# Weight conversion in lagged stages, a later P2, and two sums moved to VectorE, in a fused attention and FFN kernel

## The chip, the cores and the metric

The kernel runs on one core of one Trainium2 chip. The metric is the time of one execution on the device in microseconds (us), the median of several runs. The core has five engines that matter here: TensorE (PE, with its weight loads as PEld), VectorE (DVE), ScalarE (ACT), GpSimd (POOL) and SyncE (SP), which here only issues DMAs.

## The reference

Attention with normalised queries and keys, and then a feed-forward layer with squared ReLU:

```
q_n, k_n = rmsnorm(q) * g_q, rmsnorm(k) * g_k         # (8, 12, 448, 64) f32
attn = softmax(q_n @ k_n.T / sqrt(64))
x = (attn @ v) laid out as (8 * 448, 768)
h = maximum(x @ w_in, 0.0)                            # w_in (768, 2048)
out = (h * h) @ w_out                                 # w_out (2048, 768)
```

w_in and w_out arrive as float64; q, k, v and the output are float32.

## The kernel before

The work is cut into four units of two batches. The order of all instructions is written out by hand (`tc.manual_schedule`), and each engine executes its own in that order; the waits between engines come from the tiles that they share. A unit has 48 steps. A step belongs to one pair of heads i (12 pairs in a unit, 4 steps n = 0 to 3 in a pair) and issues the scores and exponentials of pair i (`weigh`, lines 205 and 207) and the products with the values of pair i - 1 (`attend`, line 260, with the row sums on line 267 or 271 and their reciprocal `rden` on line 282). Around these stand `normalize` for pair i + 2 (lines 156 to 166: the mean squares `ms` on DVE, the power `rr` and the product `qn` on POOL), `turn` for pair i + 1 (transposes on line 185, then `qT` on DVE at n = 0 and `kT` on ACT at n = 2) and `finish` for pair i - 2 (`xT` on line 292). Where batch 1 of a unit reaches its last three pairs, `finish` also makes the forms T1 to T4 of x (`make_x_forms`, line 317).

In unit 0 attention runs alone and the weights are converted beside it: 64 pieces of 384 KB, four to every three steps. `convert(n)` does three things: `join_words(n - 1)` (three DVE operations, lines 558 to 566), `load_weights(n + 4)` (one DMA into `words`, seven buffers) and `split_words(n)` (three ACT operations, lines 541 to 548, and a clamp on POOL, line 542). Whenever the fourth piece of a tile of weights is joined, `make_weight_forms` issues four chained sums on POOL (line 583) and one DMA on SP that writes the tile with its sums to DRAM (`in_forms`, `out_forms`, line 584). Pieces come as two tiles of w_in, two of w_out, and so on.

From step 4 of units 1, 2 and 3 on, the FFN of the unit before is spread between the attention steps (`ffn`, paced by `spent`); that of the last unit stands alone at the end. It is a Strassen-Winograd scheme with seven products for each 2 by 2 block. In each of four blocks, two tiles of `first_products` (line 383; seven products of six matmul instructions each) fill `hid`, where `hidden` adds on DVE (402), applies ReLU on ACT (403) and squares on POOL (404); then `second_products` does the rows that both batches share (line 420, 16 matmul instructions), makes four sums of `hid` on POOL (line 438), and runs three row tiles of seven products (line 448). Four PSUM banks, `roles`, take the products: P1, P6 and P7 use role 0, P5 and P3 role 1, P2 role 2, P4 role 3. `turn_roles` gives the next tile the banks of the old roles 2, 3, 1, 0 in this order, so that the next P1 writes the bank that held P2. The other banks are 0 and 1 for scores, 2 for transposes and row sums and 3 for the products with the values; in unit 0 attention has all eight.

At the end of each FFN `store` issues 14 DMAs on SP, ahead of the loads of the next unit.

Of the kernel before, what the change touches and what calls it, by code (L numbers as in the profile page):

```python
# [1 line left out]

# [11 lines left out]
ALU = mybir.AluOpType  # L14
# [59 lines left out]
def program(ctx, tc, q, k, v, g_row, moe_w_in, moe_w_out, out, shift):  # L74
# [35 lines left out]


    pairs = [(b, c) for b in range(B) for c in range(NPAIR)]
    loaded, values, squared, normal, turned = {}, {}, {}, {}, {}
    weights, sums, dens, xts, forms = {}, {}, {}, {}, {}

    def alone(i):

        return pairs[i][0] < 2

    def load_qk(i):  # L120
        b, c = pairs[i]
# [74 lines left out]
    def weigh(i, m):  # L196

        if shift:
            return weigh_shifted(i, m)
        new_weights(i, m)  # L200
        qT, kT = turned[i, 0], turned[i, 1]
        scs = [banks[(2 * (m % 2) if alone(i) else 0) + e][:CP, 0:S] for e in range(2)]
        for e, sc in enumerate(scs):
            r = ds(e * D, D)
            nc.tensor.matmul(sc, lhsT=kT[r, ts(m, CP)], rhs=qT[r, :], start=True, stop=True)  # L205
        for e, sc in enumerate(scs):
            nc.scalar.activation(  # L207
                weights[i, e, m], sc, AF.Exp, scale=normal[i][2][:, 2 * m + e : 2 * m + e + 1]
            )
        add_up(i, m)  # L210
# [35 lines left out]
                add_up(i, n)  # L246

    def values_bank(i):
        return banks[4 + i % 2 if alone(i) else 3][:, 0:S]

    def attend(i, m):

        av = values_bank(i)
        den = banks[6 + i % 2 if alone(i) else 2][:, 0:S]
        for e in range(2):
            nc.tensor.matmul(  # L260
                av[ds(e * D, D), :], lhsT=values[i][:, e, m, :], rhs=weights[i, e, m],
                start=m == 0, stop=m == NJ - 1,
            )
        for e in range(2):
            wT = weights.pop((i, e, m))
            if alone(i):
                nc.tensor.matmul(
                    den[ds(e * D, D), :], lhsT=ones, rhs=wT, start=m == 0, stop=m == NJ - 1
                )
            elif m == 1:  # L270
                nc.tensor.matmul(  # L271
                    den[ds(e * D, D), :], lhsT=ones, rhs=sums.pop((i, e)), start=True, stop=True
                )
        if m == (NJ - 1 if alone(i) else 1):
            rden = att.tile([P, S], F32, name="rden", tag="rden", bufs=1)
            if shift:
                nc.vector.tensor_scalar(
                    out=rden, in0=den, scalar1=1e-9, scalar2=None, op0=ALU.add
                )
                nc.vector.reciprocal(out=rden, in_=rden)  # L280
            else:
                nc.vector.reciprocal(out=rden, in_=den)  # L282
            dens[i] = rden
# [28 lines left out]
    def make_x_forms(u, c):  # L312
        b11, b12, b21, b22 = [xts.pop((2 * u + e, c + NK * a)) for a in range(2) for e in range(2)]
        t1, t2, t4 = new_x(), new_x(), new_x()
        t3 = b12
        for dst, left, right in (t1, b12, b11), (t2, b22, t1), (t3, b22, b12), (t4, t2, b21):
            nc.gpsimd.tensor_tensor(out=dst, in0=left, in1=right, op=ALU.subtract)
        forms[u, c] = {"11": b11, "21": b21, "22": b22, "T1": t1, "T2": t2, "T3": t3, "T4": t4}

    IN = ["11", "12", "S3", "22", "S1", "S2", "S4"]  # L320
# [21 lines left out]
    def turn_roles():  # L342
# [1 line left out]
        roles[:] = w, y, v_, x  # L344


    ORDER = [
        ("P1", 0, True, "11", "11"), ("P5", 1, True, "S1", "T1"), ("P2", 2, True, "12", "21"),
        ("P6", 0, False, "S2", "T2"), ("P4", 3, True, "22", "T4"), ("P3", 1, False, "S4", "22"),
        ("P7", 0, False, "S3", "T3"),  # L350
    ]
    COST_IN, COST_OUT = 12 * NK // 2, 10
    COST = NF // 2 * 7 * COST_IN + NBLK * (NT * 7 + 4) * COST_OUT

# [19 lines left out]
    def first_products(u, p, hid):  # L374

        turn_roles()
        n = u * NF // 2 + p
        w_sb = in_sb.pop(n)
        copies = {}
        for name, role, first, left, right in ORDER:  # L380
            ps = roles[role][:, 0:S]
            for c in range(NK):
                nc.tensor.matmul(  # L383
                    ps, lhsT=w_sb[:, c, IN.index(left), :], rhs=forms[u, c][right],
                    start=first and c == 0, stop=c == NK - 1,
                    skip_group_check=not first,
                )
            if name in ("P1", "P5", "P6", "P4"):
                copies[name] = ffn_p.tile([P, S], F32, name="part", tag="part", bufs=4)
                nc.scalar.copy(copies[name], ps)  # L390
            elif name == "P2":
                hidden(hid[0][:, 0], ps, copies["P1"], ALU.add)
            elif name == "P3":
                hidden(hid[0][:, 1], ps, copies["P6"], ALU.add)
            elif name == "P7":
                hidden(hid[1][:, 0], ps, copies["P4"], ALU.subtract)
                hidden(hid[1][:, 1], ps, copies["P5"], ALU.add)
                load_in(n + 2)
            yield COST_IN

    def hidden(dst, ps, part, op):
# [4 lines left out]
    def second_products(u, blk, hid, accs):  # L406
# [4 lines left out]
        ns = [u * NF // 2 + 2 * blk + t for t in range(2)]  # L411
        w_sb = [out_sb[n] for n in ns]


        turn_roles()
        for half in range(2):
            ps = roles[half][:, 0:HALF]
            for a in range(2):
                for t in range(2):
                    nc.tensor.matmul(  # L420
                        ps, lhsT=flat[a][:, t, ds(FULL, P)], rhs=w_sb[t][:, 2 * a + half, :],
                        start=a == 0 and t == 0, stop=a == 1 and t == 1,
                    )
            add_to(accs[-1][:, ts(half, HALF)], ps, blk == 0)
            yield 2 * COST_OUT

        sums_ = [
            ffn_p.tile([P, 2, FULL], F32, name="sums", tag=f"S{n}", bufs=1) for n in range(3)
        ]
# [1 line left out]
        a11, a12 = [a[:, :, lower] for a in flat]  # L431
        a21, a22 = [a[:, :, upper] for a in flat]
        s3 = a21
        for dst, left, right, op in (
            (s1, a21, a22, ALU.add), (s2, s1, a11, ALU.subtract),
            (s3, a11, a21, ALU.subtract), (s4, a12, s2, ALU.subtract),
        ):
            nc.gpsimd.tensor_tensor(out=dst, in0=left, in1=right, op=op)  # L438
        lefts = {"11": a11, "12": a12, "22": a22, "S1": s1, "S2": s2, "S3": s3, "S4": s4}
        for tt in range(NT):  # L440
            turn_roles()
            upper_acc, lower_acc = accs[2 * tt], accs[2 * tt + 1]
            c11, c12 = [upper_acc[:, ts(h, HALF)] for h in range(2)]
            c21, c22 = [lower_acc[:, ts(h, HALF)] for h in range(2)]
            for name, role, first, left, right in ORDER:
                ps = roles[role][:, 0:HALF]
                for t in range(2):
                    nc.tensor.matmul(  # L448
# [47 lines left out]

    def weight_pieces():

        for blk in range(NBLK):
            for p in range(2 * blk, 2 * blk + 2):  # L500
                for form, (a, b) in enumerate(((0, 0), (1, 0), (0, 1), (1, 1))):
                    yield "in", p, form, moe_w_in[ds(a * HALF, HALF), ts(p + b * NF // 2, P)]
            for t in range(2 * blk, 2 * blk + 2):
                for form in range(4):
                    a, b = divmod(form, 2)
                    yield "out", t, form, moe_w_out[ts(t + a * NF // 2, P), ts(b, HALF)]

    all_pieces = list(weight_pieces())
    words, low_words, targets = {}, {}, {}

    def target(n):
        kind, t, form, rows = all_pieces[n]
# [61 lines left out]
    def make_weight_forms(kind, dst, t):  # L574
        add, sub = ALU.add, ALU.subtract
        if kind == "in":
            a11, a12, a21, a22, s1, s2, s4 = [dst[:, :, n, :] for n in range(7)]
            todo = (s1, a21, a22, add), (s2, s1, a11, sub), (a21, a11, a21, sub), (s4, a12, s2, sub)
        else:
            b11, b12, b21, b22, t1, t2, t3, t4 = [dst[:, n, :] for n in range(8)]  # L580
            todo = (t1, b12, b11, sub), (t2, b22, t1, sub), (t3, b22, b12, sub), (t4, t2, b21, sub)
        for to, left, right, op in todo:
            nc.gpsimd.tensor_tensor(out=to, in0=left, in1=right, op=op)  # L583
        nc.sync.dma_start((in_forms if kind == "in" else out_forms)[t], dst)

    def convert(n):

        join_words(n - 1)
        load_weights(n + 4)
        split_words(n)  # L590

    load_qk(0)
    for n in range(2):
# [12 lines left out]

    last = len(pairs) - 1
    unit_steps = 2 * NPAIR * NJ  # L610

    with tc.manual_schedule(engines=ENGINES):
# [8 lines left out]
        for i, (b, c) in enumerate(pairs):  # L621
            u = b // 2
            for n in range(NJ):
# [6 lines left out]
                    load_qk(i + 3)  # L630
                if step == NJ and u:
                    stream, spent = ffn(u - 1), 0
                    if u == 1:
                        for t in range(2):
                            load_in(t)
                            load_out(t)
                while u and (
                    shift and step == NJ and spent < COST
                    or spent * (unit_steps - NJ) < COST * (step - NJ + 1)
# [15 lines left out]
                if u == 0:  # L655
                    while 3 * piece < 4 * (step + 1):
                        convert(piece)
                        piece += 1
                elif u == 1 and step == 0:
                    convert(piece)  # L660
            if b % 2 and c == NPAIR - 1:
                for _ in stream:
                    pass
# [37 lines left out]
```

## Time and profile before

| what | value |
|---|---|
| median of 3 runs | 1765.96 us (1765.89 to 1767.84) |
| the profiled execution | 1768.41 us |
| its span, first to last instruction | 1766.5 us |
| busy, share of span: PE, POOL, DVE, ACT | 89%, 40%, 42%, 31% |
| mean granted TensorE clock | 0.952 of full |

The trace is of one execution. Busy times of one engine may overlap a little with its idle times, because the ends of matmuls are modelled. A granted clock of 1.00 is 2.4 GHz, and 0.50 is 1.2 GHz.

### The profile page before, as it was taken

How to read it: one execution, taken by the hardware profiler on the slowest of the kernel's cores; microseconds unless marked ns; L12 is line 12 of the kernel's file. 1: busy time of each engine (PE TensorE's matmuls, PEld its weight loads, DVE VectorE, ACT ScalarE, POOL GpSimd, SP SyncE). 2: the span in 40 equal slices, each digit the busy share in tenths (PEclk: the TensorE clock that was granted, in tenths of full speed). 3: DMA queues.
4: the chain of work that ended last, by engine and by line, in shares of the span. 5: the costliest groups of instructions: out<-in, count | busy, mean ns of one | idle time of the engine just before them, and what ended most of it. 6: DMA issues, size and time to landing. Idle time of an engine off the chain costs nothing.

```text
span 1766.5 us, 15113 instructions
## 1 busy us (share of the span) xinstructions
PE 1578.4 (89%) x5204; PEld 718.9 (41%) x5204; DVE 747.0 (42%) x1082; ACT 551.8 (31%) x1033; POOL 708.2 (40%) x578
## 2 busy tenths in 40 slices
PE   4766765999998989999998989999998999999997
PEld 1222212444444433444444434344443444555554
DVE  3666665333434435233534435234434544113223
ACT  4656653333132222333231322233222221220110
POOL 4555557334324354434424344533524253312312
PEclk9888887999999999999999999999999999999999
DMA  4677665203131314113131313213231223122112
GB/s 145 215 231 223 214 216 200 105 27 134 47 119 53 129 47 158 55 47 129 52 118 47 121 57 128 89 47 118 63 119 47 87 73 133 64 102 103 63 72 65
DMA packets 101081, 188.25 MB, mean 107 GB/s; under 512 B 49284, under 2 KB 83076, under 8 KB 90756
## 3 DMA queue, kind: packets, MB, share of 16 engines
q1 hardware_dynamic: 100992, 187.20, 31.3%
q8 instruction: 43, 0.70, 0.2%
q14 instruction: 42, 0.34, 0.1%
q10 hardware_dynamic: 4, 0.00, 0.0%
HBM read 152.57 MB, written 34.60 MB: 106 GB/s over the span
## 4 chain that ended last, share of the span: by engine, by line
PE 73%; POOL 11%; DVE 6%; issue 5%; DMA 2%; ACT 2%; SPq 1%; POOLq 0%; DVEq 0%; ACTq 0%
PE bank L383 28%; PE bank L448 25%; PE bank L205 8%; PE bank L260 7%; PE bank L420 3%; POOL rr L161 3%; PE bank L185 2%; POOL hid L404 2%; PE bank L271 1%; DVE rden L282 1%; POOL in_sb L583 1%; DMA out_dram<-acc 1%; POOL out_sb L583 1%; POOL words L542 1%; POOL sum L223 1%
## 5 line engine op out<-in xcount | busy, mean ns | idle before, releaser
L383 PE MATMUL bank<-xT,in_sb 128*128 128x448 f32 x1344 | 531.2, 550 | 21.0 <-DMA in_sb<-in_forms 13.1
L207 ACT ACTIVATE wT<-bank,rr 112x448 f32<-112x448 f32 x384 | 221.3, 627 | 505.9 <-PE bank L205 482.4
L383 PEld LDWEIGHTS bank<-xT,in_sb 128*128 128x128 f32 x1344 | 252.6, 192 | 274.4 <-issue 239.9
L404 POOL TENSOR_TENSOR hid<-hid 128x448 f32<-128x448 f32 x128 | 119.1, 941 | 576.8 <-ACT hid L403 576.8
L480 DVE TENSOR_TENSOR acc<-acc,bank 128x384 f32<-128x384 f32 x324 | 173.6, 550 | 273.5 <-PE bank L448 176.9
L205 PE MATMUL bank<-qT,kT 64*112 64x448 f32 x768 | 218.8, 626 | 76.5 <-DVE qT L187 72.9
L448 PE MATMUL bank<-out_sb,hid 128*128 128x384 f32 x768 | 275.6, 488 | 0.0
L161 POOL TENSOR_TENSOR rr<-ms,minus_half 112x16 f32<-112x16 f32 x48 | 150.1, 3128 | 273.8 <-DVE ms L157 266.8
L448 PE MATMUL bank<-out_sb,sums 128*128 128x384 f32 x576 | 215.7, 498 | 19.1 <-POOL sums L438 19.1
L402 DVE TENSOR_TENSOR hid<-bank,part 128x448 f32<-128x448 f32 x128 | 76.5, 618 | 348.9 <-PE bank L383 325.7
L260 PE MATMUL bank<-wT,vt 112*64 112x448 f32 x768 | 197.4, 595 | 3.7 <-DVE xT L292 3.7
L448 PEld LDWEIGHTS bank<-out_sb,hid 128*128 128x128 f32 x768 | 145.8, 191 | 104.0 <-issue 6.4
L282 DVE RECIPROCAL rden<-bank 128x448 f32<-128x448 f32 x48 | 141.9, 2956 | 102.6 <-PE bank L271 102.6
L390 ACT COPY part<-bank 128x448 f32<-128x448 f32 x128 | 68.1, 532 | 302.8 <-PE bank L383 302.8
L448 PEld LDWEIGHTS bank<-out_sb,sums 128*128 128x128 f32 x576 | 106.1, 192 | 103.8 <-POOL sums L438 22.8
L403 ACT ACTIVATE hid<-hid 128x448 f32<-128x448 f32 x128 | 72.3, 577 | 239.7 <-DVE hid L402 239.7
L205 PEld LDWEIGHTS bank<-qT,kT 64*112 64x112 f32 x768 | 60.7, 185 | 195.0 <-issue 81.6
L420 PE MATMUL bank<-out_sb,hid 128*128 128x384 f32 x256 | 95.9, 521 | 31.5 <-POOL hid L404 31.5
L223 DVE TENSOR_TENSOR sum<-sum,wT 112x448 f32<-112x448 f32 x72 | 76.9, 1068 | 77.1 <-ACT wT L207 73.8
L223 POOL TENSOR_TENSOR sum<-sum,wT 112x448 f32<-112x448 f32 x72 | 81.7, 1135 | 64.3 <-ACT wT L207 61.4
L260 PEld LDWEIGHTS bank<-wT,vt 112*64 112x64 f32 x768 | 39.8, 140 | 142.1 <-issue 126.8
L420 PEld LDWEIGHTS bank<-out_sb,hid 128*128 128x128 f32 x256 | 50.4, 202 | 76.0 <-POOL hid L404 41.3
(52 smaller groups left out, 1087.7 us busy)
## 6 DMA issues: line engine op xcount, KB each, us to landing
out_sb<-out_forms SPq DMA_DIRECT2D x32, 1536.0 KB, 9.3
in_sb<-in_forms SPq DMA_DIRECT2D x32, 1344.0 KB, 5.8
words<-in_moe_w_in_dram SPq DMA_DIRECT2D x32, 384.0 KB, 7.2
words<-in_moe_w_out_dram SPq DMA_DIRECT2D x32, 384.0 KB, 6.4
out_forms<-out_sb SPq DMA_DIRECT2D x8, 1536.0 KB, 6.5
qk<-in_q_dram SPq DMA_DIRECT2D x48, 224.0 KB, 2.8
qk<-in_k_dram SPq DMA_DIRECT2D x96, 112.0 KB, 3.0
vt<-in_v_dram SPq DMA_DIRECT2D x48, 224.0 KB, 3.2
```

The source lines that it names most:

```text
L161: nc.gpsimd.tensor_tensor(out=rr.rearrange("p x r -> p (x r)"), in0=ms, in1=minus_half.to_broadcast([CP, 4 * NJ]), op=ALU.pow,)
L205: nc.tensor.matmul(sc, lhsT=kT[r, ts(m, CP)], rhs=qT[r, :], start=True, stop=True)
L207: nc.scalar.activation(weights[i, e, m], sc, AF.Exp, scale=normal[i][2][:, 2 * m + e : 2 * m + e + 1])
L223: engine.tensor_tensor(out=sums[i, e], in0=sums[i, e], in1=weights[i, e, m], op=ALU.add)
L260: nc.tensor.matmul(av[ds(e * D, D), :], lhsT=values[i][:, e, m, :], rhs=weights[i, e, m], start=m == 0, stop=m == NJ - 1,)
L282: nc.vector.reciprocal(out=rden, in_=den)
L383: nc.tensor.matmul(ps, lhsT=w_sb[:, c, IN.index(left), :], rhs=forms[u, c][right], start=first and c == 0, stop=c == NK - 1, skip_group_ch ...
L402: nc.vector.tensor_tensor(out=dst, in0=ps, in1=part, op=op)
L404: nc.gpsimd.tensor_tensor(out=dst, in0=dst, in1=dst, op=ALU.mult)
L420: nc.tensor.matmul(ps, lhsT=flat[a][:, t, ds(FULL, P)], rhs=w_sb[t][:, 2 * a + half, :], start=a == 0 and t == 0, stop=a == 1 and t == 1,)
L448: nc.tensor.matmul(ps, lhsT=lefts[left][:, t, ts(tt, P)], rhs=w_sb[t][:, OUT.index(right), :], start=first and t == 0, stop=t == 1, skip_g ...
L480: nc.vector.tensor_tensor(out=acc, in0=acc, in1=ps, op=ALU.add)
```

## The change

The conversion pipeline gets three pieces of lag: `convert(n)` joins piece n - 3, loads piece n + 4 (into the buffer that this join releases), splits piece n, and issues one POOL sum from a queue in place of four at once. Tiles of w_in and w_out alternate. What the lag leaves over, and the first loads of the FFN's weights, stand in step 0 of unit 1. P2 becomes the last product in the first layer; its second layer keeps the order. S1 and S2 move to DVE and ahead of the shared rows, S4 and S3 stay on POOL with S4 first; the shared rows start with the second half of `hid`. T1 and T2 move to DVE. At the first pair of units 1, 2 and 3, scores of odd steps go to banks 4 and 6, and the pair before uses banks 5 and 7.

```diff
+    def between(i):
+        return pairs[i][0] % 2 == 0 and pairs[i][1] == 0
...
-        scs = [banks[(2 * (m % 2) if alone(i) else 0) + e][:CP, 0:S] for e in range(2)]
+        odd = (2, 3) if alone(i) else (4, 6) if between(i) else (0, 1)
+        scs = [banks[odd[e] if m % 2 else e][:CP, 0:S] for e in range(2)]
...
     def values_bank(i):
-        return banks[4 + i % 2 if alone(i) else 3][:, 0:S]
+        apart = i < last and between(i + 1)
+        return banks[4 + i % 2 if alone(i) else 5 if apart else 3][:, 0:S]
+
+    def sums_bank(i):
+        apart = i < last and between(i + 1)
+        return banks[6 + i % 2 if alone(i) else 7 if apart else 2][:, 0:S]
...
-        for dst, left, right in (t1, b12, b11), (t2, b22, t1), (t3, b22, b12), (t4, t2, b21):
-            nc.gpsimd.tensor_tensor(out=dst, in0=left, in1=right, op=ALU.subtract)
+        for engine, dst, left, right in (
+            (nc.vector, t1, b12, b11), (nc.gpsimd, t3, b22, b12),
+            (nc.vector, t2, b22, t1), (nc.gpsimd, t4, t2, b21),
+        ):
+            engine.tensor_tensor(out=dst, in0=left, in1=right, op=ALU.subtract)
...
+    FIRST_ORDER = ["P1", "P5", "P6", "P4", "P3", "P7", "P2"]
+    SECOND_ORDER = ["P1", "P5", "P2", "P6", "P4", "P3", "P7"]
...
             elif name == "P2":
                 hidden(hid[0][:, 0], ps, copies["P1"], ALU.add)
+                load_in(n + 2)
...
-                load_in(n + 2)
             yield COST_IN
...
-        for dst, left, right, op in (
-            (s1, a21, a22, ALU.add), (s2, s1, a11, ALU.subtract),
-            (s3, a11, a21, ALU.subtract), (s4, a12, s2, ALU.subtract),
+        for engine, dst, left, right, op in (
+            (nc.vector, s1, a21, a22, ALU.add), (nc.vector, s2, s1, a11, ALU.subtract),
+            (nc.gpsimd, s4, a12, s2, ALU.subtract), (nc.gpsimd, s3, a11, a21, ALU.subtract),
         ):
-            nc.gpsimd.tensor_tensor(out=dst, in0=left, in1=right, op=op)
+            engine.tensor_tensor(out=dst, in0=left, in1=right, op=op)
+
+        turn_roles()
+        for half in range(2):
+            ps = roles[half][:, 0:HALF]
+            for a in (1, 0):
...
+        order = [("in", 0), ("in", 1)]
+        for n in range(NF // 2):
+            order.append(("out", n))
+            if n + 2 < NF // 2:
+                order.append(("in", n + 2))
...
+    words, low_words, targets, sums_to_make = {}, {}, {}, deque()
+    LAG = 3
...
-        for to, left, right, op in todo:
+        sums_to_make.extend(todo)
+        sums_to_make.append(((in_forms if kind == "in" else out_forms)[t], dst))
+
+    def make_sum():
+
+        if sums_to_make:
+            to, left, right, op = sums_to_make.popleft()
             nc.gpsimd.tensor_tensor(out=to, in0=left, in1=right, op=op)
-        nc.sync.dma_start((in_forms if kind == "in" else out_forms)[t], dst)
+            if len(sums_to_make[0]) == 2:
+                nc.sync.dma_start(*sums_to_make.popleft())
 
     def convert(n):
 
-        join_words(n - 1)
-        load_weights(n + 4)
+        join_words(n - LAG)
+        load_weights(n + 2 * NT - LAG + 1)
         split_words(n)
+        make_sum()
...
                 if step == NJ and u:
                     stream, spent = ffn(u - 1), 0
-                    if u == 1:
-                        for t in range(2):
-                            load_in(t)
-                            load_out(t)
...
                 elif u == 1 and step == 0:
-                    convert(piece)
+                    while piece < len(all_pieces) + LAG or sums_to_make:
+                        convert(piece)
+                        piece += 1
+                    for t in range(2):
+                        load_in(t)
+                        load_out(t)
```

## Rows read from the trace of the kernel before

**Rows 1.** Windows by stage: length, busy us of each engine, granted clock, DMA share, GB/s
```profile
24.00:257.00 233.00, 160.38 (x592) 50.97 (x592) 151.21 (x234) 149.43 (x295) 129.06 (x136) 0.82 0.64 209
...
303.00:689.00 386.00, 368.96 (x1221) 170.38 (x1222) 155.93 (x219) 108.50 (x199) 146.48 (x108) 0.98 0.25 85
...
1494.00:1766.50 272.50, 256.62 (x738) 139.43 (x736) 69.77 (x124) 41.84 (x78) 61.40 (x51) 0.99 0.24 86
```

**Rows 2.** Waits in unit 0, 24 to 257 us: total, times, longest
```profile
DVE out_sb L558 <- POOL words L542: 38.9, 10, 6.8
...
DVE in_sb L558 <- POOL words L542: 31.9, 8, 4.6
```

**Rows 3.** Timeline of PE, first scores of a pair in unit 0, three pairs apart
```profile
173.30 1.84 PE L205 MATMUL bank<-qT,kT 64*112 64x448 f32 x4 [9.53 <-DVE qT L187]
...
238.16 1.84 PE L205 MATMUL bank<-qT,kT 64*112 64x448 f32 x4 [9.53 <-DVE qT L187]
```

**Rows 4.** DMA issues in 150 to 257 us: median us from issue to landing
```profile
words<-in_moe_w_in_dram SPq DMA_DIRECT2D x12, 384.0 KB, 8.0
```

**Rows 5.** Timeline of DVE and POOL near the end of unit 0
```profile
257.95 0.56 DVE L562 SCALAR_TENSOR_TENSOR out_sb<-words,out_sb 128x384 uint32<-128x384 uint32 x1
...
259.88 3.74 POOL L317 TENSOR_TENSOR xT<-xT 128x448 f32<-128x448 f32 x3 [5.46 <-DVE xT L292]
...
261.26 1.37 DVE L562 SCALAR_TENSOR_TENSOR out_sb<-words,out_sb 128x384 uint32<-128x384 uint32 x1
```

**Rows 6.** Groups by line, whole span: busy us, mean ns
```profile
L583 POOL TENSOR_TENSOR out_sb<-out_sb 128x384 f32<-128x384 f32 x32 | 32.8, 1047 | 35.0 <-DVE out_sb L566 34.9
```

**Rows 7.** Timeline from unit 0 to the first FFN
```profile
281.56 0.62 DVE L292 TENSOR_TENSOR xT<-bank,rden 128x448 f32<-128x448 f32 x1
...
291.20 0.35 SPq L584 DMA_DIRECT2D out_forms<-out_sb  x1
...
295.67 0.55 SPq L333 DMA_DIRECT2D in_sb<-in_forms  x1
...
303.19 9.63 PE L383 MATMUL bank<-xT,in_sb 128*128 128x448 f32 x18 [13.14 <-DMA in_sb<-in_forms]
```

**Rows 8.** Waits of PE in 303 to 1494 us, by line
```profile
L448 PE MATMUL bank<-out_sb,sums 128*128 128x384 f32 x432 | 163.4, 501 | 19.1 <-POOL sums L438 19.1
...
L420 PE MATMUL bank<-out_sb,hid 128*128 128x384 f32 x192 | 73.5, 530 | 26.0 <-POOL hid L404 26.0
```

**Rows 9.** Timeline around 700 us: where an FFN starts
```profile
690.98 0.97 PE L260 MATMUL bank<-wT,vt 112*64 112x448 f32 x4 [0.80 <-DVE xT L292]
...
698.17 0.60 PE L185 MATMUL bank<-ident,qk 112*128 112x112 f32 x4 [1.24 <-DVE rden L282]
...
700.54 4.03 PE L383 MATMUL bank<-xT,in_sb 128*128 128x448 f32 x10
...
708.49 4.10 PE L383 MATMUL bank<-xT,in_sb 128*128 128x448 f32 x5 [3.93 <-POOL xT L317]
```

**Rows 10.** Timeline from first to second products, FFN alone
```profile
1525.67 2.10 PE L420 MATMUL bank<-out_sb,hid 128*128 128x384 f32 x6
...
1525.95 1.16 DVE L402 TENSOR_TENSOR hid<-bank,part 128x448 f32<-128x448 f32 x2 [1.63 <-PE bank L383]
...
1527.26 1.82 POOL L404 TENSOR_TENSOR hid<-hid 128x448 f32<-128x448 f32 x2 [1.32 <-ACT hid L403]
...
1529.14 3.49 PE L420 MATMUL bank<-out_sb,hid 128*128 128x384 f32 x10 [1.36 <-POOL hid L404]
```

**Rows 11.** Chain that ended last, blocks 3 and 4 of unit 1
```profile
531.52 3.21 POOL rr L161
...
539.97 5.19 PE bank L420 x10
...
649.50 4.67 PE bank L448 x8
656.01 6.65 PE bank L448 x20
```

More of the change, by code (lines that the diff above doesn't have):

```diff
@@ L1 @@
+from collections import deque
 from contextlib import ExitStack
@@ L112, in program @@
     pairs = [(b, c) for b in range(B) for c in range(NPAIR)]
+    last = len(pairs) - 1
     loaded, values, squared, normal, turned = {}, {}, {}, {}, {}
@@ L248, in values_bank @@
     def values_bank(i):
-        return banks[4 + i % 2 if alone(i) else 3][:, 0:S]
+        apart = i < last and between(i + 1)
[3 more added lines that the diff above has]
+        return banks[6 + i % 2 if alone(i) else 7 if apart else 2][:, 0:S]
     def attend(i, m):
         av = values_bank(i)
-        den = banks[6 + i % 2 if alone(i) else 2][:, 0:S]
+        den = sums_bank(i)
         for e in range(2):
@@ L344, in turn_roles @@
         roles[:] = w, y, v_, x
[L347 to L351, printed above, removed]
+    PRODUCTS = {
+        "P1": (0, True, "11", "11"), "P2": (2, True, "12", "21"), "P3": (1, False, "S4", "22"),
+        "P4": (3, True, "22", "T4"), "P5": (1, True, "S1", "T1"), "P6": (0, False, "S2", "T2"),
+        "P7": (0, False, "S3", "T3"),
+    }
+    FIRST_ORDER = ["P1", "P5", "P6", "P4", "P3", "P7", "P2"]
+    SECOND_ORDER = ["P1", "P5", "P2", "P6", "P4", "P3", "P7"]
     COST_IN, COST_OUT = 12 * NK // 2, 10
@@ L379, in first_products @@
         copies = {}
-        for name, role, first, left, right in ORDER:
+        for name in FIRST_ORDER:
+            role, first, left, right = PRODUCTS[name]
             ps = roles[role][:, 0:S]
@@ L412, in second_products @@
         w_sb = [out_sb[n] for n in ns]
[L415 to L418, printed above, removed]
-                for t in range(2):
[L420 to L425, printed above, removed]
         sums_ = [
@@ L433, in second_products @@
         s3 = a21
-        for dst, left, right, op in (
-            (s1, a21, a22, ALU.add), (s2, s1, a11, ALU.subtract),
-            (s3, a11, a21, ALU.subtract), (s4, a12, s2, ALU.subtract),
-        ):
-            nc.gpsimd.tensor_tensor(out=dst, in0=left, in1=right, op=op)
+        for engine, dst, left, right, op in (
+            (nc.vector, s1, a21, a22, ALU.add), (nc.vector, s2, s1, a11, ALU.subtract),
+            (nc.gpsimd, s4, a12, s2, ALU.subtract), (nc.gpsimd, s3, a11, a21, ALU.subtract),
+        ):
+            engine.tensor_tensor(out=dst, in0=left, in1=right, op=op)
[4 more added lines that the diff above has]
+                for t in range(2):
+                    nc.tensor.matmul(
+                        ps, lhsT=flat[a][:, t, ds(FULL, P)], rhs=w_sb[t][:, 2 * a + half, :],
+                        start=a == 1 and t == 0, stop=a == 0 and t == 1,
+                    )
+            add_to(accs[-1][:, ts(half, HALF)], ps, blk == 0)
+            yield 2 * COST_OUT
         lefts = {"11": a11, "12": a12, "22": a22, "S1": s1, "S2": s2, "S3": s3, "S4": s4}
@@ L444, in second_products @@
             c21, c22 = [lower_acc[:, ts(h, HALF)] for h in range(2)]
-            for name, role, first, left, right in ORDER:
+            for name in SECOND_ORDER:
+                role, first, left, right = PRODUCTS[name]
                 ps = roles[role][:, 0:HALF]
@@ L497, in weight_pieces @@
     def weight_pieces():
[L499 to L504, printed above, removed]
+        order = [("in", 0), ("in", 1)]
[3 more added lines that the diff above has]
+                order.append(("in", n + 2))
+        for kind, t in order:
+            for form in range(4):
+                if kind == "in":
+                    b, a = divmod(form, 2)
+                    yield kind, t, form, moe_w_in[ds(a * HALF, HALF), ts(t + b * NF // 2, P)]
+                else:
                     a, b = divmod(form, 2)
-                    yield "out", t, form, moe_w_out[ts(t + a * NF // 2, P), ts(b, HALF)]
+                    yield kind, t, form, moe_w_out[ts(t + a * NF // 2, P), ts(b, HALF)]
     all_pieces = list(weight_pieces())
-    words, low_words, targets = {}, {}, {}
+    words, low_words, targets, sums_to_make = {}, {}, {}, deque()
+    LAG = 3
     def target(n):
@@ L604, in program @@
     make_identity(nc, ident)
-    last = len(pairs) - 1
     unit_steps = 2 * NPAIR * NJ
@@ L632, in program @@
                     stream, spent = ffn(u - 1), 0
-                    if u == 1:
-                        for t in range(2):
-                            load_in(t)
-                            load_out(t)
                 while u and (
@@ L659, in program @@
                 elif u == 1 and step == 0:
-                    convert(piece)
+                    while piece < len(all_pieces) + LAG or sums_to_make:
+                        convert(piece)
+                        piece += 1
+                    for t in range(2):
+                        load_in(t)
+                        load_out(t)
             if b % 2 and c == NPAIR - 1:
```

## The prediction

> **What bounds the kernel now.** I read the windows by stage first. There are two regimes. In unit 0 no engine is full: of 233 us PE is busy for 160 (at a granted clock of 0.82), DVE 151, ACT 149 and POOL 129, and the DMA share is 0.64. From 303 us on PE is the bound: 369 of 386 us in unit 1, 257 of 272 in the FFN that stands alone [rows 1]. So in unit 0 waits between engines set the time, and later each idle stretch of PE costs its own length.
>
> The timeline of PE in unit 0 gives the pace. The first scores of a pair come at 173.30 and, three pairs later, at 238.16: 21.62 us a pair, and both wait some 9.5 us for DVE's `qT` [rows 3]. DVE is late because of the conversion: the joins wait 38.9 + 31.9 = 70.8 us for POOL's clamp [rows 2], which stands on POOL behind four chained sums that themselves need the last join. Divided by the 233 / 21.62 = 10.8 pairs in the window, the busy times are 14.0 us a pair on DVE, 13.8 on ACT, 12.0 on POOL, 14.9 on PE, and 13.8 of full DMA. Nothing is above 14.9 of 21.6.
>
> After that I listed PE's waits from 303 to 1494 us. The largest are 26.0 us on line 420 for the squares of `hid`, and 19.1 on line 448 for the sums [rows 8]. The rest stand where an FFN begins: 13.14 us for `in_sb` in unit 1 [rows 7] and 3.93 us for T1 in units 2 and 3 [rows 9].
>
> **The change, part by part.**
>
> *Conversion.* With a lag of three pieces a join finds its clamp and its low words done long before, and POOL does one sum between two clamps. The 70.8 us of waits lose their cause. The number of operations stays, so the pair falls from 21.62 us towards the busiest engine. The lower bound is PE's 14.9, or DVE's 14.0 plus two joins stretched by POOL as in [rows 5], 1.5: 15.5. The upper bound is today's 21.6. In between stands a loop, that of the buffers: seven tiles of `words`, of which three now wait in the lag, so that a load, the split and the join (seven operations of some 0.56 us [rows 5], 4 us, an estimate) go round in four pieces. With the 8.0 us from issue to landing [rows 4] a piece takes (8 + 4) / 4 = 3.0 us, and the 5.33 pieces of a pair 16.0; a landing of 10 us would make it 18.7. Four resources between 14 and 16 us that wait for each other in order won't all be full; I take 18.0 us a pair, between this loop at 8 and at 10 us of landing. Over 12 pairs that is (21.62 - 18.0) x 12 = 43 us gained, with 73 and 0 as ends.
>
> DVE's operations with two SBUF inputs stretch beside POOL: the join on line 562 took 0.56 us alone and 1.37 beside POOL's line 317 [rows 5]. If DVE had to sit out each of the 5.33 sums of 1.05 us [rows 6], that would add 5.6 us: 19.6 a pair, a gain of 24 instead of 43. It is a rival below. The Trainium skill, "SBUF — State Buffer", section "Who interferes with whom", speaks against the change here: a DVE instruction with two SBUF inputs contends with a GpSimd instruction that reads SBUF, and whichever starts first holds the shared pair for its whole length. The trace agrees with it as far as those two rows go. By that rule S1 and S2 would also wait for squares on POOL, which the slack named below covers.
>
> *From unit 0 to the first FFN.* The loads of `in_sb` are issued in step 0, no longer in step 4, and I yet count nothing. On SP they stand behind the last form write, and that now ends a longer tail: after `finish` (`xT`, T1, T2, `qT`: 2.5 to 4.5 us on DVE) come three joins (nine operations of 0.56 us, 5 us, or up to 9 if each is stretched as in [rows 5]), then four sums (4.2 us [rows 6], up to 5), so that the write is issued 12 to 18 us after this `finish`, and the load, which shares the DMA engines with it, lands some 9 us later: 21 to 27. Today it is 303.19 - 281.56 = 21.6 us, with write and load issued at 291.20 and 295.67 [rows 7]. Two of these joins were part of unit 0 before (3.5 us less there), so the net is 0, from +5 to -13 (the load entirely hidden).
>
> *P2 last.* This has a price. The next P1 writes P2's bank. Where the FFN stands alone, the last slot of line 383 ends at 1525.67, DVE starts at 1525.95 and needs 0.58 us for each `hid`, and PE follows a POOL result within 0.06 us [rows 10]. So PE waits 0.28 + 0.58 + 0.06 = 0.92 us at every change from the first tile to the second: 16 times. Between the attention steps the pieces of stream are 3, 3, 2, 3, 2 and 1 products, so the change falls inside a piece and no attention step covers it; in three blocks a reciprocal stands in front on DVE and adds 0.45. Price: 14.7 + 1.4 = 16 us.
>
> At the second change, from the second tile to the shared rows, it gives something back. Alone, PE runs six of the sixteen matmuls and then waits 1.36 us for the two squares of P7 [rows 10]. Afterwards P2's square is done 0.28 + 1.31 + 0.91 + 0.06 = 2.56 us after its matmuls (DVE to POOL 1.31 us in the same rows). The bank opens at 0.92, and six matmuls take 2.10, to 3.02: the square is no longer waited for. It is 0.92 in place of 1.36 to 1.7 at 13 places. In the third block of each unit nothing improves: there the squares wait behind `rr` and two sums on POOL (531.52, line 420 resumes at 539.97 [rows 11]), and P2's square will. Gain about 5 us, taken from 26.0 and four times 1.36. P2 last alone therefore loses 11 us; its bounds are 0 (DVE reads the bank sooner than the rows say) and 30.
>
> *S1 and S2 on DVE.* They are issued before the shared rows and before the attention step that now comes between. P5, which reads S1, comes after sixteen matmuls of line 420 (over 5 us), so the 19.1 us [rows 8] go. Twice the matmuls behind this wait were slow: eight matmuls of line 448 took 4.67 us where twenty take 6.65 [rows 11], that is 2.0 us more each time. Gain 23. DVE waits for P2's square before S2; queued behind it are the adds of the shared rows, which need line 420 anyway, and the next attention's `qT`, which has a step of slack. No row has DVE at 768 columns; from 0.58 us at 448 [rows 10] it is at least 1 us, and 3 with a POOL operation sat out. Either is inside the 5 us.
>
> *T1 and T2 on DVE, free banks.* T1 follows `xT` on DVE at once, and the 3.93 us go twice; the five matmuls after it took 4.10 us where ten took 4.03 before it [rows 9], so 2.1 more go each time. Gain 12. The waits of 0.80 for bank 3 and of 1.24 for bank 2 [rows 9] go with banks 5 and 7, at two changes of unit: 4. Both can be at most these, and no less than nothing.
>
> **Sum.** 43 + 0 - 16 + 5 + 23 + 12 + 4 = 71 us off the span of 1766.5: 1695.5. Its execution took 1768.4, 1.9 more than the span, and the median of the runs lies 2.4 below that execution: 1695 us.
>
> **Rivals.**
> 1. *The port*: DVE waits out POOL's sums as worked out above, 19.6 us a pair: 1714. For it speaks the 1.37 us; against, that such pairs of rows are few in unit 0. Chance 0.15. This is the rule of the Trainium skill's page "SBUF — State Buffer" carried through.
> 2. *The loads*: the buffer loop, with landing above 12 us, keeps unit 0 at today's pace, the change's first aim not reached: 1738. A load is now issued only when the join three pieces back is done; for it speaks the DMA share of 0.64 at a fifth less pace; against, landings of 8.0 us. Chance 0.12.
> 3. *The busiest engine*: 15.5 us a pair, or 1665. PE's 14.9 is at a clock of 0.82 and would shrink. Chance 0.13.
> 4. *Slower*: P2's bank is handed on 32 times (16 to the second tile, 16 to the shared rows). If DVE stood behind a whole reciprocal (2.96 us) at each, they would cost 32 x 2.96 = 95 us: 1790. It decides from 71 / 32 = 2.2 us each. Against it, a reciprocal precedes in only three of twelve blocks. Chance 0.05.
>
> The forecast has 0.50; 0.05 is left for what I don't see, on either side.
>
> **The range** takes in rivals 1 and 3 and the hidden load, and rival 2: 1665 to 1738. The bound between a change and none is 0.2%, 3.5 us; all cases but the slow one and part of the rest are below it: faster 0.92, same 0.03, slower 0.05.
>
> **What would show it.** Right: the first scores of pairs in unit 0 about 18 us apart; no wait of joins for the clamp; PE waiting some 0.9 us for `hid` of line 402 at line 383, sixteen times, and at line 420; no wait on line 448 for sums, none for T1; a wait for `in_sb` of some 10 us before the first FFN. Wrong: pairs 21 us apart with ACT waiting for `words`; joins of line 562 above 1 us on average; PE's wait for P2's bank above 2 us; an FFN in unit 1 that starts without a wait.

## The result and the profile after

The changed kernel takes 1700.1 us (median of four runs, 1699.2 to 1700.9) where the kernel before took 1766.5 in the same session: a ratio of 0.9623, interval 0.9606 to 0.964. It is 66 us faster; 71 had been forecast. Its profiled execution took 1700.4 us, with a span of 1698.6. Of the six runs of one experiment, P2 third again, one took 2658.8 us at a granted clock of 0.559 and is left out; the only trace of that experiment is of this run, so the waits with P2 third are read from the last experiment.

Below are the windows by stage of the changed kernel (columns as in [rows 1]): unit 0, the FFN of unit 1 with attention, and the FFN alone.

```profile
24.00:250.00 226.00, 174.21 (x652) 55.13 (x652) 183.00 (x257) 160.49 (x318) 149.81 (x147) 0.87 0.71 227
...
271.40:640.00 368.60, 358.61 (x1190) 164.86 (x1192) 156.78 (x221) 106.18 (x195) 125.70 (x94) 0.99 0.25 88
...
1423.80:1698.60 274.80, 258.21 (x738) 138.77 (x736) 79.11 (x134) 41.84 (x78) 48.41 (x42) 0.99 0.23 85
```

DVE is now busy for 81% of unit 0 (65% in [rows 1]). The FFN alone became 2.3 us longer (274.8 for 272.5), which is P2's doing, as the experiments on P2 show.

The starts of the four FFNs on PE cut the gain into stages. In order, the changed kernel's timeline of PE has:

```profile
271.45 3.89 PE L402 MATMUL bank<-xT,in_sb 128*128 128x448 f32 x5 [11.49 <-DMA in_sb<-in_forms]
...
658.20 7.03 PE L402 MATMUL bank<-xT,in_sb 128*128 128x448 f32 x18 [0.34 <-ACT wT L214]
...
1041.71 7.03 PE L402 MATMUL bank<-xT,in_sb 128*128 128x448 f32 x18 [0.34 <-ACT wT L214]
...
1423.81 16.05 PE L402 MATMUL bank<-xT,in_sb 128*128 128x448 f32 x42
```

Before, they started at 303.19 [rows 7], 700.54 [rows 9], 1103.25 and 1494.00. So the way to the first FFN is 31.7 us shorter, and the three stretches from one FFN to the next are 10.6, 19.2 and 8.7 us shorter; with 2.3 lost at the end that makes the 67.9 between the spans. No `xT` wait of 3.93 us is left where an FFN starts.

The waits of PE in the changed kernel, longest first (total, times, longest; lines 212, 402, 451 and 468 are 205, 383, 420 and 448 of before):

```profile
PE bank L212 <- DVE qT L193: 43.0, 12, 6.0
PE bank L191 <- POOL qn L172: 13.9, 3, 9.1
PE bank L451 <- POOL hid L423: 13.1, 7, 3.4
PE bank L402 <- DVE hid L421: 12.7, 16, 1.1
PE bank L402 <- DMA in_sb<-in_forms: 11.5, 1, 11.5
PE bank L451 <- DVE hid L421: 7.6, 9, 1.1
...
PE bank L451 <- POOL sum L230: 2.3, 3, 0.8
```

The wait for the sums of `hid` (19.1 us in [rows 8]) is gone. In its place stands the forecast one: sixteen times on line 402 for DVE to read P2's bank. The load of `in_sb` is still waited for.

Unit 0 did not reach its forecast pace. The first scores of PE behind DVE's `qT`, nine pairs apart:

```profile
56.40 1.71 PE L212 MATMUL bank<-qT,kT 64*112 64x448 f32 x4 [3.19 <-DVE qT L193]
...
230.46 1.69 PE L212 MATMUL bank<-qT,kT 64*112 64x448 f32 x4 [4.48 <-DVE qT L193]
```

That is 19.34 us a pair: 21.62 before [rows 3], 18.0 forecast, 19.6 under the rival of the port. (The last of these pairs are longer, because `finish` also makes forms of x there; over six earlier pairs it is 19.1, as given below.) What happens in one pair is read from the timelines of DVE and PE:

```profile
202.59 2.96 DVE L294 RECIPROCAL rden<-bank 128x448 f32<-128x448 f32 x1 [2.97 <-PE bank L279]
...
210.13 0.68 DVE L193 TENSOR_SCALAR qT<-bank,g 128x448 f32<-128x448 f32 x1
...
210.86 1.84 PE L212 MATMUL bank<-qT,kT 64*112 64x448 f32 x4 [5.19 <-DVE qT L193]
...
222.93 2.96 DVE L294 RECIPROCAL rden<-bank 128x448 f32<-128x448 f32 x1 [2.48 <-PE bank L279]
```

The two engines take turns. From the reciprocal at 202.59 to the end of `qT` at 210.81 DVE needs 8.2 us (the reciprocal, two joins, `xT` and `qT`; 5.8 in pairs with one join there). PE waits 5.19 us for the end of this `qT`. It does not need it as an operand yet: `qT` of pair i + 1 is made in step 0 of pair i, and the scores that wait are those of step 1 of pair i, and not its first ones, as the heading of [rows 3] calls them. They go to bank 2, from which DVE reads the transposes for `qT`. PE then runs three steps, some 12 us, and DVE, which has meanwhile run out of joins, waits 2.48 us for the last of them before its next reciprocal. Of the joins no wait for the clamp is left.

### The profile page after: what moved, and what is told of

Read it like the earlier page. It is cut to its first block, busy times and chain, and to the rows that moved or that the text cites. A ratio compares the mean times of both kernels' runs of the same rounds, so it can differ in the third digit from the quotient of the medians.

```text
span 1698.6 us, 15053 instructions
## 1 busy us (share of the span) xinstructions
PE 1567.1 (92%) x5204; PEld 710.7 (42%) x5204; DVE 794.4 (47%) x1138; ACT 552.1 (33%) x1033; POOL 643.9 (38%) x522
## 4 chain that ended last, share of the span: by engine, by line
PE 82%; DVE 6%; POOL 5%; issue 4%; DMA 2%; ACT 2%; SPq 0%; POOLq 0%; DVEq 0%; ACTq 0%
PE bank L402 28%; PE bank L468 26%; PE bank L212 9%; PE bank L272 8%; PE bank L451 5%; PE bank L191 2%; PE bank L283 2%; POOL rr L167 2%; DVE rden L294 1%; DVE hid L421 1%; PE bank L279 1%; POOL hid L423 1%; DVE out_sb L588 1%; ACT wT L214 1%; DMA in_sb<-in_forms 1%
## 5 line engine op out<-in xcount | busy, mean ns | idle before, releaser
L402 PE MATMUL bank<-xT,in_sb 128*128 128x448 f32 x1344 | 528.0, 545 | 24.8 <-DVE hid L421 12.7
L402 PEld LDWEIGHTS bank<-xT,in_sb 128*128 128x128 f32 x1344 | 249.0, 190 | 280.0 <-issue 247.9
L468 PE MATMUL bank<-out_sb,hid 128*128 128x384 f32 x768 | 274.6, 487 | 0.0
L468 PEld LDWEIGHTS bank<-out_sb,hid 128*128 128x128 f32 x768 | 144.7, 190 | 103.1 <-issue 5.3
L230 DVE TENSOR_TENSOR sum<-sum,wT 112x448 f32<-112x448 f32 x72 | 65.1, 904 | 140.0 <-ACT wT L214 137.1
L451 PE MATMUL bank<-out_sb,hid 128*128 128x384 f32 x256 | 91.5, 510 | 23.1 <-POOL hid L423 13.1
L230 POOL TENSOR_TENSOR sum<-sum,wT 112x448 f32<-112x448 f32 x72 | 87.8, 1220 | 59.3 <-ACT wT L214 56.2
L193 DVE TENSOR_SCALAR qT<-bank,g 128x448 f32<-128x448 f32 x48 | 32.7, 682 | 120.1 <-PE bank L191 120.1
```

Source lines behind the costliest of these rows:

```text
L230: engine.tensor_tensor(out=sums[i, e], in0=sums[i, e], in1=weights[i, e, m], op=ALU.add)
L402: nc.tensor.matmul(ps, lhsT=w_sb[:, c, IN.index(left), :], rhs=forms[u, c][right], start=first and c == 0, stop=c == NK - 1, skip_group_ch ...
L451: nc.tensor.matmul(ps, lhsT=flat[a][:, t, ds(FULL, P)], rhs=w_sb[t][:, 2 * a + half, :], start=a == 1 and t == 0, stop=a == 0 and t == 1,)
L468: nc.tensor.matmul(ps, lhsT=lefts[left][:, t, ts(tt, P)], rhs=w_sb[t][:, OUT.index(right), :], start=first and t == 0, stop=t == 1, skip_g ...
```

## Experiments

Ratios are to the kernel before, timed in the same session; the changed kernel's is 0.9623. One per cent is 17.7 us.

### Unit 0: a loop through bank 2, or the port

**Other banks for the transposes of unit 0.** In steps of unit 0 the banks of row sums and values of the pair before last are free.

```diff
-        tr = banks[2 + x if alone(i) else 2][:, 0:S]
+        tr = banks[6 - 2 * x + (i - 1) % 2 if alone(i) else 2][:, 0:S]
```

> The transposes of unit 0 go to the banks of the row sums and of the values that are free between two pairs, no longer to banks 2 and 3 of the odd scores. In the changed kernel a pair of unit 0 takes 19.3 us, where 18.0 was forecast. Loop theory: PE runs only three steps past the transposes (some 12 us) until the scores of the next pair's odd step need bank 2, which DVE's qT holds; DVE in turn needs those three steps for its reciprocal, and then takes some 7.5 us to the next qT. With other banks the loop opens: a pair of 16 to 17 us, the first FFN 25 to 35 us earlier than 271, a median of 1665 to 1675. Port theory (DVE stretched by POOL's sums sets the pair): no more than 5 us, 1695 to 1700.

Measured: 1683.5 us, ratio 0.9531 (0.9515 to 0.9547). The gain of 16 us is half of what the loop theory asked for and three times what the port theory allowed. In unit 0 DVE's wait for PE before its reciprocal falls from 27.1 us to 1.5, PE's wait for `qT` from 43.0 to 5.5, and DVE is busy for 190 of 208 us. A smaller wait comes in: PE's transposes wait 12.7 us for the reciprocal, which reads the bank that they now use. And DVE's joins grow. The groups by line of DVE in 24 to 230 us, first of the changed kernel, then of this one:

```profile
L588 DVE SCALAR_TENSOR_TENSOR in_sb<-words,in_sb 128x384 uint32<-128x384 uint32 x32 | 21.9, 685 | 1.1
L592 DVE CUSTOM_DVE_ANT_0 in_sb<-in_sb,low 128x768 uint16<-128x768 uint16 x32 | 21.1, 658 | 3.4 <-ACT words L567 0.6 <-ACT squares L154 0.5
```

```profile
L592 DVE CUSTOM_DVE_ANT_0 in_sb<-in_sb,low 128x768 uint16<-128x768 uint16 x32 | 26.3, 823 | 3.8 <-ACT words L572 0.6
L588 DVE SCALAR_TENSOR_TENSOR in_sb<-words,in_sb 128x384 uint32<-128x384 uint32 x32 | 23.7, 741 | 1.1
```

So the loop was real, and opening it made DVE the bound, at operations that grow beside POOL.

**Memsets in place of the conversion's sums,** alone and together with the other banks.

```diff
-            nc.gpsimd.tensor_tensor(out=to, in0=left, in1=right, op=op)
+            nc.gpsimd.memset(to, 0.0)
```

> Leaves out the sums of the weight conversion: each POOL sum is a memset of the same tile, which reads no SBUF, so the output is not the reference's. Port theory: the joins on lines 588 and 592 fall back from 0.69 to 0.80 us towards 0.56, DVE has 1 to 1.5 us less a pair, and since DVE sets the pair it comes down from 19.3 to 17.5 or less: some 20 us. Loop theory: only the joins between the reciprocal and qT shorten, at most 1 us a pair: 0 to 12 us, and PE still waits for qT at each pair.

> Both edits: memsets for the sums of the conversion (output not the reference's) and other banks for the transposes of unit 0. If the loop hides the port, the memsets are worth more here than alone: with the loop open DVE is the busiest engine (15.7 us a pair), so that 1 to 1.5 us a pair, 12 to 18 us, come on top of the banks' gain. If the port is no bound with the loop open either, no more than 5 us on top, and the loads or ACT (14 us a pair) are next.

Measured: 1672.7 us for the memsets alone, 1658.0 for both (one run each; the runs of one kernel elsewhere here lie 0.2 to 4.2 us apart): 27 and 42 us less than the changed kernel. On top of the banks the memsets are worth as much as alone (26 us), more than either theory gave them, so the loop does not hide them: both have a share, and the shares add. By `qT` on DVE a pair takes 19.11 us in the changed kernel ((170.31 - 55.66) / 6), 17.58 with the banks, 17.06 with the memsets and 15.60 with both. This is over six pairs of unit 0, because the pieces fall on the steps in the same way every three pairs. Beside the memsets the joins of the changed kernel are back at about their length alone:

```profile
L592 DVE CUSTOM_DVE_ANT_0 in_sb<-in_sb,low 128x768 uint16<-128x768 uint16 x32 | 18.5, 577 | 3.4 <-ACT words L567 0.6 <-ACT wT L214 0.5
L588 DVE SCALAR_TENSOR_TENSOR in_sb<-words,in_sb 128x384 uint32<-128x384 uint32 x32 | 18.0, 562 | 1.1
```

A memset takes 0.42 us and a sum 1.08, so that a mean could fall just because less of POOL's time lies beside the joins. Single joins decide it. First one beside a sum in the changed kernel, then one beside a memset:

```profile
56.96 1.30 POOL L615 TENSOR_TENSOR in_sb<-in_sb 128x384 f32<-128x384 f32 x1
57.44 1.24 DVE L592 CUSTOM_DVE_ANT_0 out_sb<-out_sb,low 128x768 uint16<-128x768 uint16 x1
...
70.70 0.42 POOL L615 MEMSET out_sb<- 128x384 f32 x1
70.84 0.56 DVE L588 SCALAR_TENSOR_TENSOR in_sb<-words,in_sb 128x384 uint32<-128x384 uint32 x1
```

In the changed kernel the 17 joins that overlap a sum and no other operation of POOL take 1.00 to 1.24 us, and the 55 that overlap nothing 0.56. In the two runs with memsets the 8 joins that overlap a memset alone take 0.56.

The Trainium skill, "SBUF — State Buffer", section "Who interferes with whom", says that a DVE instruction with two SBUF inputs contends with a GpSimd instruction that reads SBUF and not with one that only writes it. The 0.56 us beside memsets, where it was 1.00 to 1.24 beside sums, agree. For one reader it does not show: the 23 joins of the changed kernel beside line 167 alone (`rr`, 112x16, which POOL reads from SBUF too) take 0.56 us as well.

With the loop open, DVE's shorter operations account for the gain of the memsets: its busy time falls from 16.6 us a pair to 14.6 (1.8 of it in the joins), and the pair by as much (17.58 to 15.60). With the loop closed the account has a gap. Over both kinds of tile the joins are 0.29 us a piece shorter, 1.5 us a pair, not all of them in DVE's half of the loop, and the pair shrank by 2.1. Two other things changed beside them and were not separated: POOL's own time is shorter, and PE's 336 matmuls of the six pairs were busy for 83.3 us at a granted clock of 0.90, where they were 88.2 at 0.85 (means over the two levels, 0.50 and 1.00).

**The old conversion under the rest of the change.** Lag one, four sums at once, two tiles of a kind after each other, loads in step 4:

```diff
-        sums_to_make.extend(todo)
...
+        for to, left, right, op in todo:
             nc.gpsimd.tensor_tensor(out=to, in0=left, in1=right, op=op)
...
-        join_words(n - LAG)
-        load_weights(n + 2 * NT - LAG + 1)
+        join_words(n - 1)
+        load_weights(n + 4)
         split_words(n)
-        make_sum()
...
```

> The changed kernel with the conversion of before: lag of one, four sums at once, the old order of pieces, loads of the FFN in step 4. All the rest of the change stays. Forecast: the conversion was worth 43 us of the 71, so 1743. By the start of the first FFN in the two traces (303.19 and 271.45 us) it is worth 32: 1732. Rival, that moving P2 and the sums is worth less than the rest of the trace says: above 1745.

Measured: 1730.7 us, ratio 0.98 (0.9783 to 0.9816). The conversion is worth 31 us, as the starts of the first FFN before and after said (303.19 and 271.45), not 43.

### From unit 0 to the first FFN

**The loads of `in_sb` ahead of the remaining conversions.**

```diff
+                    for t in range(2):
+                        load_in(t)
                     while piece < len(all_pieces) + LAG or sums_to_make:
                         convert(piece)
                         piece += 1
                     for t in range(2):
-                        load_in(t)
                         load_out(t)
```

> The two loads of in_sb are issued at the start of step 0 of unit 1, ahead of the remaining conversions, not behind the last form write. Theory: PE's wait of 11.5 us before the first FFN comes from SP's order, the load standing behind the last form write; it goes, and with it 2 us of slow matmuls after it: 1687 to 1690. Rival: the wait is DMA bandwidth, or T1 and the last xT come hardly earlier than the load: 1695 to 1700.

Measured: 1692.8 us, ratio 0.9587 (0.9572 to 0.9601), 6 to 7 us less than the changed kernel; 10 to 13 had been expected. In the changed kernel SP issues the last two form writes and then the load:

```profile
254.81 7.50 SPq L617 DMA_DIRECT2D out_forms<-out_sb  x2
262.36 0.42 SPq L348 DMA_DIRECT2D in_sb<-in_forms  x1
```

The load lands at 271.3. With the load ahead, PE's timeline has:

```profile
256.29 2.52 PE L402 MATMUL bank<-xT,in_sb 128*128 128x448 f32 x6
...
263.52 7.14 PE L402 MATMUL bank<-xT,in_sb 128*128 128x448 f32 x12 [4.71 <-DVE rden L294]
```

and that of DVE:

```profile
260.51 2.95 DVE L294 RECIPROCAL rden<-bank 128x448 f32<-128x448 f32 x1
263.50 0.62 DVE L304 TENSOR_TENSOR xT<-bank,rden 128x448 f32<-128x448 f32 x1
```

The wait for the load is gone and P1 runs, 15 us earlier. P5 then waits 4.71 us. It goes on 0.06 us after the end of the reciprocal (263.46), when the last `xT` has only begun, so it does not wait for that pair's T1. By the kernel's turn of banks P5 of the first FFN writes bank 7, which holds the row sums that this reciprocal reads. SP's order was the cause of the old wait, and a shared bank behind DVE's tail of unit 0 is next; other banks here were not tried.

### P2

**P2 third again,** with the shared rows starting at the first half of `hid`:

```diff
-    FIRST_ORDER = ["P1", "P5", "P6", "P4", "P3", "P7", "P2"]
+    FIRST_ORDER = ["P1", "P5", "P2", "P6", "P4", "P3", "P7"]
...
-            for a in (1, 0):
+            for a in (0, 1):
...
```

> Undoes the later P2 alone: P2 third again in the first layer, and the shared rows start with the first half of hid. S1 and S2 stay on DVE. Forecast, by its terms of 16 lost and 5 won: 11 us faster than the changed kernel, 1689. By the waits in the changed kernel's trace (12.7 us for P2's bank at line 402, and 23 for line 451 where the old order had 31.5): 4 us faster, 1696. Rival, the later P2 is what lets S1 and S2 on DVE pay: slower, 1705 or more, with PE waiting at line 468 for sums.

Measured: 1693.0 us, ratio 0.9581 (0.9568 to 0.9594). The later P2 costs 7 us, between the two sizes expected. The rival is out: the run is faster, so S1 and S2 on DVE pay without the later P2.

**P2 last with another turn of the banks,** so that the next P1 gets P4's bank:

```diff
+    def turn_after_p2():
+        x, v_, w, y = roles
+        roles[:] = y, v_, w, x
...
-        turn_roles()
+        turn_after_p2()
```

The new turn stands at the head of `first_products` and ahead of the shared rows.

> P2 stays last, but the first layer and the shared rows take the banks in another turn: the next P1 gets the bank of P4, not that of P2. Theory: the price of the later P2 is the wait for its bank alone. PE's 12.7 us at line 402 go, and at line 451 the 7.6 us for line 421; there P2's square is then waited for with some 0.4 us at 13 places. Expected 1700 - 12.7 - 3 = 1684, below the 1693 of P2 in third place. Rival: the waits move to the squares on POOL, and the later P2 gives nothing: 1693 or more.

Measured: 1686.9 us, ratio 0.9545 (0.9532 to 0.9558): 14 us less than the changed kernel and 6 less than with P2 third. Lines 402 and 451 are 406 and 455 here; nothing waits for P2's bank any more:

```profile
PE bank L455 <- POOL hid L427: 20.6, 20, 4.3
```

The price of the later P2 was its bank. The later P2 itself is a gain of some 6 us. It shows in the FFN that stands alone, too: 274.8 us in the changed kernel, 272.5 before (with P2 third) and 271.2 here. The new turn has a price of its own where an FFN starts. It gives P1 of the second FFN the bank that attention's last values are still read from, and PE waits there:

```profile
PE bank L406 <- DVE xT L304: 2.7, 1, 2.7
```

### The sums and the forms

**S1 and S2 back on POOL,** behind the shared rows (the four sums of the diff, all with `nc.gpsimd`, after the loop over `half`):

> S1 and S2 back on POOL and behind the shared rows. Forecast: the sums were worth 23 us, so 1723, with PE waiting some 19 us in total at line 468 for sums. Rival: with P2 last, POOL's squares come in another order, and the wait does not come back: 1705 or less.

Measured: 1725.7 us, ratio 0.977 (0.9755 to 0.9785): worth 26 us. The wait comes back nearly in full:

```profile
PE bank L467 <- POOL sums L456: 18.8, 6, 6.8
```

**T1 and T2 back on POOL:**

```diff
-            (nc.vector, t1, b12, b11), (nc.gpsimd, t3, b22, b12),
-            (nc.vector, t2, b22, t1), (nc.gpsimd, t4, t2, b21),
+            (nc.gpsimd, t1, b12, b11), (nc.gpsimd, t2, b22, t1),
+            (nc.gpsimd, t3, b22, b12), (nc.gpsimd, t4, t2, b21),
```

> T1 and T2 back on POOL. Forecast: worth 12 us at the starts of units 2 and 3's FFNs, so 1712. Rival: since attention at the change of units now has banks of its own, PE reaches the FFN earlier and the wait for T1 is longer, 20 us or more: 1720.

Measured: 1715.3 us, ratio 0.9713 (0.9698 to 0.9727): worth 16 us. PE's wait for `xT` is 4.83 us at each of two changes of unit, longer than the 3.93 of [rows 9]: the rival's direction at a smaller size. That PE arrives earlier at this place, with banks of its own ahead of it, fits but was not tried apart.

```profile
1060.06 5.36 PE L402 MATMUL bank<-xT,in_sb 128*128 128x448 f32 x8 [4.83 <-POOL xT L332]
```

**The banks between units shared again** (odd scores in banks 0 and 1, values and sums in 3 and 2):

> Undoes the free banks between units alone: scores of odd steps in banks 0 and 1 again, the pair before on banks 3 and 2. Forecast: worth 4 us at two changes of unit, so 1704, with PE's waits of 0.8 for xT and 1.2 for the reciprocal back at each. Rival: with T1 on DVE the FFN no longer waits for POOL, and PE's waits ahead of it count fully, with the first change of unit too: 1706 or more; or they are covered: 1700.

Measured: 1706.9 us, ratio 0.9656 (0.9643 to 0.9669): worth 6 us. The two waits are back in its trace:

```profile
PE bank L272 <- DVE xT L304: 3.6, 3, 2.1
PE bank L191 <- DVE rden L294: 2.5, 2, 1.2
```

With the 2.1 us that the changed kernel has on line 272 as well, these are 4.0 us more.

### Three edits together

**Other turn of the banks, load ahead, other banks for the transposes,** on the changed kernel:

> The changed kernel with three edits together: the turn of banks after P2, the loads of in_sb ahead of the remaining conversions, and the transposes of unit 0 in other banks. If they add up: 1700 - 16 - 7 - 17 = 1660. If the transposes' banks and the earlier load share a gain (DVE's tail of unit 0 then bounds the first FFN), 1665 to 1670.

Measured: 1664.1 us, ratio 0.9415 (0.9402 to 0.9428). It beats both kernels, by 36 us over the changed one and 103 over the one before. The single edits sum to 36 (14 + 6 + 16), so they add up. The first FFN still starts with a wait, now for DVE's reciprocal:

```profile
244.21 2.95 DVE L294 RECIPROCAL rden<-bank 128x448 f32<-128x448 f32 x1
...
247.22 9.17 PE L406 MATMUL bank<-xT,in_sb 128*128 128x448 f32 x18 [7.14 <-DVE rden L294]
```

It ends 0.06 us after the reciprocal. With this turn it is P1, not P5, that gets bank 7, so the first product already waits for the row sums of unit 0 to be read.

**The same with P2 third and the old turn:**

> As the version with three edits, but with P2 in third place and the old turn of banks, to see its waits in a trace and whether a later P2 with the other turn is worth its place. By adding up what the single edits gave: 1700 - 7.4 - 6.4 - 16.2 = 1670, 6 us slower than with P2 last and the other turn (1664). In the trace: no wait at line 402 for line 421; at line 451 some 31 us for the squares on POOL, as before the change. Rival: the wait at line 451 is much smaller than 31 us, because POOL no longer has S1 and S2, and P2 last is then worth nothing: 1664 or less.

Measured: 1668.1 us, ratio 0.9438 (0.9425 to 0.9451). P2 last with the right bank is worth 4 us here. The wait for squares is what it was before the change, 26.0 in units 1 to 3 [rows 8] and four times 1.36 [rows 10]:

```profile
PE bank L451 <- POOL hid L423: 31.5, 16, 4.3
```

## Why the prediction was right, and where it missed

It gave 1695 us and faster; 1700.1 came. The mechanisms of the change hold, but the sum owes part of its closeness to luck: the conversion gave 12 us less than forecast, and the other terms together, each measured alone, some 13 more.

- **Conversion, forecast 43, measured 31.** This term failed in size. The step was "Four resources between 14 and 16 us that wait for each other in order won't all be full; I take 18.0 us a pair". Measured were 19.1 to 19.3. The 18.0 came from the buffer loop, and that was no bound: `words` landed in some 4.4 us in the changed kernel (median of the whole run, 6.4 and 7.2 before), not in the 8 to 10 assumed. That 18.0 came near the pace is therefore luck. What held the pair up were two other things. One is the turn-taking of PE and DVE through bank 2 (1.5 us a pair, by the other banks): [rows 3] showed PE waiting for `qT` at each pair, and I put that wait down to the joins alone. The other is the port: its rival's pace of 19.6 was nearly met, though DVE sat out far less than all of each sum (the memsets give 2.1 us a pair, part of it perhaps for other reasons, against the 5.6 of the rival). With both taken away a pair took 15.6 us, near the prediction's lower bound of 15.5. Rival 2, the loads, is out, and so is rival 3 for this kernel.
- **From unit 0 to the first FFN, forecast 0 net.** Right within 2 us. From the `xT` of the same `finish` to line 402 it takes 271.45 - 248.24 = 23.2 us (21.6 before), inside the 21 to 27 forecast, and 11.5 of them are a wait for the load behind the form write.
- **P2, forecast -16 and +5, measured -7.** Right in mechanism. PE's waits for the bank are 12.7 us in sixteen: thirteen of 0.72 and three of 1.1 with a reciprocal in front. The 0.92 had 0.28 us between the last matmul and DVE, of which 0.03 is left (the ends of matmuls are modelled). That another turn of the banks takes this price away, the prediction did not see. At line 451 the waits fell from 31.5 to 23.0, by 8.5 and not 5. The slower rival's price per change was never near 2.2 us.
- **S1 and S2, forecast 23, measured 26; T1 and T2, forecast 12, measured 16; banks, forecast 4, measured 6.** All right in mechanism and a little small. For T1 and T2 the wait itself was longer in its run (4.83 us); for the other two no run tells the reason.

The single terms measured (31, -7, 26, 16 and 6) sum to 72, the whole is 66. Each ratio is uncertain by 2 to 3 us, and the 6 us between were not followed further.

## What to carry to other kernels

When an order of products is changed, follow the buffers too: the same reorder cost 7 us with the banks turned the old way and gained 4 to 6 with another turn. Where no engine is full, taking away the longest wait leaves the next loop; look in the trace for two engines that wait for each other in turn, and for the buffer that joins them. A transfer that is moved ahead in program order isn't earlier while a waiting issue stands before it on the same queue.

## What the runs showed of the hardware

DVE's joins with two SBUF inputs took 0.56 to 0.59 us with POOL's sums replaced by memsets, 0.66 to 0.77 beside the sums in the changed kernel (means by line and kind of tile), and up to 0.82 once DVE ran with few pauses: the stretch grew as the rest got better. With memsets and the other banks together they took 0.61 to 0.63, so that POOL's other operations stretch them a little as well. I had expected the stretch only as a rival.
